# Two linear-attention and SwiGLU layers: gate and up of four column groups by two nested levels of seven block products instead of one

## The chip, the core and the metric

The kernel runs on one core of one Trainium2 chip, in one launch. The metric is the device time of a run in microseconds (us), as the median of several runs. Engine names are those of the profile: PE (TensorE matmuls), PEld (its weight loads), DVE (VectorE), ACT (ScalarE), POOL (GpSimd), SP (SyncE, which issues every DMA of this kernel). L947 is line 947 of the kernel's file.

## What is computed

Two equal layers are applied to x of 1 x 2048 x 512, one after the other; the weights are shared by the layers.

```python
x = x + A(layernorm(x), wqkv, wo)      # linear attention, 32 heads
x = x + B(layernorm(x), w1, w3, w2)    # SwiGLU MLP, F = 1792
x = x + A(layernorm(x), wqkv, wo)
x = x + B(layernorm(x), w1, w3, w2)

def B(x, w1, w3, w2):                  # x: 2048 x 512
    gate, up = x @ w1, x @ w3          # 512 x 1792 each
    return (silu(gate) * up) @ w2      # 1792 x 512
```

The change is in B of the second layer, "layer 1".

## The kernel before

**Numbers.** Every operand of a large matmul is held as two fp16 parts, a high part (the value rounded to fp16) and a low part (what is left). A product takes three matmul passes (`PASSES`: high x high, low x high, high x low), written by `mm` (L942, matmul at L947). So whoever makes an operand pays a rounding (ACT copy to fp16) and a subtraction (DVE or POOL, "low part").

**The MLP by seven products.** A product of two matrices, each cut into 2 x 2 blocks, can be made from seven block products instead of eight, if sums and differences of blocks stand ready on both sides (Winograd's form). P1 to P7 in the code name, for each of the seven products, which of the seven weight blocks or sums and which of the seven row blocks or sums it multiplies. Gate and up are made in this way: D = 512 is cut in two, the F columns in two, the tokens of a chunk in two. F is cut into seven **groups** (128 columns from each half of F, for w1 and for w3), the 2048 tokens into four **chunks** of 512 (as two halves of 256). The sums of weights and of rows are prepared ahead, in fp16 parts: the weights in layer 0 by `background`, a generator that is advanced a few steps after every group; the rows for each chunk by `mlp_rows` (L1963), which also writes them to DRAM (`xb_d`) for the later sets.

**A group** (`mlp_group`, L2029) is one group on one chunk: seven products x 2 weights x k = 2 x 3 passes = 84 matmuls of 128x256 into three PSUM banks, bb, ba and bc. The results are linear combinations of the products: ACT copies a bank to SBUF as it grows (L2052), DVE adds others to it (L2055, `a+`, `b+`, `c+`), so that the four quarters of gate and up arise. ACT makes the Silu (L2007) and DVE the gated product (L2008).

**The hidden values** (`hidden`, L2015) are cut for the down projection, which goes by seven products too: four sums of 128x256 (L2023 to L2026, on DVE or POOL, by a table), a high part on ACT (L2011) and a low part on DVE or POOL (L2013).

**Down** (`mlp_out`, L2087, matmul at L2097): for each group and each half of the chunk's rows, 42 matmuls of 128x256 that add up in four PSUM banks po0 to po3 over the groups of a set. At a set's end `mlp_add` (L2129) adds the banks to x: one ACT copy (L2148), five DVE operations that read po (L2146), and two adds in SBUF (L2154, L2155, on DVE or POOL by a table). The last group of all uses plain products (`mlp_out_plain`, L2106).

**Sets and slots.** `SETS` lists which groups run together; each set passes over the four chunks. Layer 0 has (0,1,2), (3,4), (5,6); layer 1 has (4,5,6), then (3,0,1,2). Prepared weights lie in SBUF slots of 14 KB (w1, w3) and 7 KB (w2) per partition; those that don't fit are written to DRAM (`store`) and fetched again (`fetch`).

**What sets the order.** In each engine the instructions run in the order of a written-out table `ORDER`, one list of numbers for each engine (PE, DVE, ACT, POOL, SP), which `arrange` (L679) imposes. So an instruction that waits holds up all that its list puts behind it. SP's list is the only DMA queue.

## Time and profile before

| | |
|---|---|
| median of 3 runs | 1136.95 us (1136.2 to 1137.05) |
| profiled execution: span | 1134.0 us |
| instructions | 22473 |
| PE busy | 1123.7 us, 9117 matmuls |
| DVE busy | 849.3 us |
| ACT busy | 663.2 us |
| POOL busy | 429.7 us |
| DMA | 162.94 MB, 144 GB/s in the mean |

The MLP of layer 0 runs from 186 to 561 us of the span, the attention of layer 1 to 753, the first set of layer 1's MLP to 904, its second set to 1109, and the last down projections to 1134. These borders are read from the adds from ba (L2055), of which there is one for each group and chunk. From 384.3 to 560.6 us are the last 13 of layer 0's 28 groups on chunks, from 752.9 to 903.7 the 12 of layer 1's first set, from 903.7 to 1108.9 the 16 of its second.

A row that groups instructions has line, engine, operation, names written and read, shapes and count, then busy us, the mean ns of one, and the engine's idle time just ahead of them with what ended it. A row of a single name or line has the shortest, median and longest duration in ns and the first and last start in us. A timeline row has start, duration (of the first start to the last end, where it stands for several), engine and operation, in brackets the idle time before it. In a table of stretches each engine's busy us stand with the number of instructions, then the granted TensorE clock, the busy share of the DMA engines and GB/s.

### The profile page before, as it was taken

How to read it: one execution, taken by the hardware profiler on the slowest of the kernel's cores; microseconds unless marked ns; L12 is line 12 of the kernel's file. 1: busy time of each engine (PE TensorE's matmuls, PEld its weight loads, DVE VectorE, ACT ScalarE, POOL GpSimd, SP SyncE). 2: the span in 40 equal slices, each digit the busy share in tenths (PEclk: the TensorE clock that was granted, in tenths of full speed). 3: DMA queues.
4: the chain of work that ended last, by engine and by line, in shares of the span. 5: the costliest groups of instructions: out<-in, count | busy, mean ns of one | idle time of the engine just before them, and what ended most of it. 6: DMA issues, size and time to landing. Idle time of an engine off the chain costs nothing.

```text
span 1134.0 us, 22473 instructions
## 1 busy us (share of the span) xinstructions
PE 1123.7 (99%) x9117; PEld 888.3 (78%) x9117; DVE 849.3 (75%) x1468; ACT 663.2 (58%) x1104; POOL 429.7 (38%) x477
## 2 busy tenths in 40 slices
PE   8999999999999999999999999999999999999998
PEld 3445446888888888888886676578888888888887
DVE  7789878896978887889896488847855666465556
ACT  7668878775544445455578666686544434343442
POOL 6731796502001222335678416862152110302113
PEclk9999999999999999999999999999999999999999
DMA  8995665389673332331267946643482440220001
GB/s 258 304 292 181 174 136 121 75 220 272 204 279 122 117 149 103 112 155 66 48 179 177 276 165 153 114 89 105 120 240 102 177 178 1 85 84 29 11 20 57
DMA packets 171768, 162.94 MB, mean 144 GB/s; under 512 B 139536, under 2 KB 147984, under 8 KB 167056
## 3 DMA queue, kind: packets, MB, share of 16 engines
q1 hardware_dynamic: 171664, 161.51, 48.7%
q8 instruction: 71, 1.16, 0.4%
q14 instruction: 33, 0.27, 0.1%
HBM read 80.08 MB, written 47.32 MB: 112 GB/s over the span
## 4 chain that ended last, share of the span: by engine, by line
PE 91%; DVE 2%; POOL 2%; DMA 2%; issue 1%; ACT 1%; SPq 0%; DVEq 0%; POOLq 0%; ACTq 0%
PE bb L947 26%; PE po L2097 20%; PE bc L947 13%; PE ba L947 6%; PE gt L947 6%; PE po L947 5%; PE pq L947 4%; PE pk L947 3%; PE po L2117 3%; DMA arena<-arena 2%; PE kb L947 1%; PE qb L947 1%; PE kc L947 1%; PE kv L947 0%; PE qc L947 0%
## 5 line engine op out<-in xcount | busy, mean ns | idle before, releaser
L947 PEld LDWEIGHTS <-arena 128*128 128x128 f16 x6648 | 646.1, 98 | 204.5 <-DMA arena<-arena 4.4
L947 PE MATMUL bb<-arena 128*128 128x256 f16 x2688 | 349.2, 273 | 0.0
L2097 PE MATMUL po<-arena 128*128 128x256 f16 x2058 | 288.5, 273 | 0.0
L2052 ACT ACTIVATE arena<-bb 128x512 f32<-128x512 f32 x196 | 115.3, 594 | 195.5 <-PE bb L947 166.7
L2097 PEld LDWEIGHTS <-arena 128*128 128x128 f16 x2058 | 201.3, 98 | 23.4
L947 PE MATMUL bc<-arena 128*128 128x256 f16 x1344 | 179.6, 273 | 0.0
L2055 DVE TENSOR_TENSOR arena<-arena,bc 128x512 f32<-128x512 f32 x112 | 76.7, 685 | 87.5 <-PE bc L947 54.1
L2007 ACT ACTIVATE arena<-arena,scalars 128x512 f32<-128x512 f32 x112 | 74.6, 666 | 90.2 <-DVE arena L2055 70.2
L2146 DVE SCALAR_TENSOR_TENSOR arena<-po,scalars,arena 128x256 f32<-128x256 f32 (+1 forms) x180 | 101.5, 585 | 31.7 <-PE po L2097 21.7
L2013 DVE TENSOR_TENSOR arena<-arena 128x1280 f16<-128x1280 f32 (+1 forms) x90 | 105.4, 1174 | 21.2 <-ACT arena L2011 20.8
L2011 ACT ACTIVATE arena<-arena 128x512 f16<-128x512 f32 (+1 forms) x112 | 101.0, 904 | 32.2 <-DVE arena L2026 13.7
L2008 DVE SCALAR_TENSOR_TENSOR arena<-arena,scalars 128x512 f32<-128x512 f32 x112 | 78.6, 705 | 34.5 <-ACT arena L2007 34.4
L947 PE MATMUL ba<-arena 128*128 128x256 f16 x672 | 91.8, 273 | 0.0
L947 PE MATMUL gt<-arena 128*128 128x512 f16 x384 | 89.6, 379 | 0.0
L947 PE MATMUL po<-arena 128*128 128x512 f16 x384 | 86.8, 379 | 0.5 <-DMA arena<-arena 0.5
L2013 POOL TENSOR_TENSOR arena<-arena 128x512 f16<-128x512 f32 x22 | 27.0, 1228 | 115.0 <-ACT arena L2011 108.2
L2155 POOL TENSOR_TENSOR arena<-arena 128x512 f32<-128x512 f32 x27 | 38.0, 1406 | 81.7 <-DVE arena L2146 81.7
L2154 POOL TENSOR_TENSOR arena<-arena 128x512 f32<-128x512 f32 x27 | 37.1, 1375 | 71.4 <-DVE arena L2146 69.3
L871 DVE SCALAR_TENSOR_TENSOR arena<-arena,scalars 128x512 f16<-128x512 f32 (+2 forms) x74 | 59.1, 814 | 2.3 <-ACT arena L869 2.2
L924 ACT ACTIVATE arena<-arena,nb_all,rs_all 128x512 f32<-128x512 f32 x64 | 50.8, 806 | 13.2 <-POOL nb_all L921 7.6
L2023 POOL TENSOR_TENSOR arena<-arena 128x256 f32<-128x256 f32 x10 | 7.9, 786 | 131.3 <-DVE arena L2008 131.3
L869 ACT ACTIVATE arena<-arena,scalars 128x512 f16<-128x512 f32 (+2 forms) x74 | 52.2, 718 | 5.2 <-DVE arena L1003 2.3
(234 smaller groups left out, 1449.4 us busy)
## 6 DMA issues: line engine op xcount, KB each, us to landing
arena<-xb_d SPq DMA_DIRECT2D x12, 1792.0 KB, 8.0
xb_d<-arena SPq DMA_DIRECT2D x8, 1792.0 KB, 7.7
w_d<-arena SPq DMA_DIRECT2D x5, 1792.0 KB, 7.6
arena<-w_d SPq DMA_DIRECT2D x5, 1792.0 KB, 8.0
arena<-in_B_w_dram SPq DMA_DIRECT2D x8, 896.0 KB, 7.0
arena<-in_B_w_dram SPq DMA_DIRECT2D x28, 256.0 KB, 3.0
xt_d<-arena SPq DMA_DIRECT2D x8, 896.0 KB, 5.1
arena<-xt_d SPq DMA_DIRECT2D x8, 896.0 KB, 6.7
```

Of the source, the lines that this page charges most:

```text
L869: nc.scalar.activation(hi, src, AF.Copy, scale=scale)
L871: lambda: nc.vector.scalar_tensor_tensor(lo, src, scale, hi, OP.mult, OP.subtract)
L924: nc.scalar.activation(dst, x_sb[:, t, :], AF.Identity, scale=rs_all[:, t : t + 1], bias=nb_all[:, t : t + 1],)
L947: nc.tensor.matmul(dst, lhs(a, k), rhs(b, k), start=first and k == 0 and i == 0, stop=last and k == n - 1 and i == len(PASSES) - 1, skip_g ...
L2007: nc.scalar.activation(t, gate, AF.Silu, scale=info["u1"])
L2008: nc.vector.scalar_tensor_tensor(t, up, info["hid"], t, OP.mult, OP.mult)
L2011: nc.scalar.activation(hs[:, 0, lo:hi], t[:, lo:hi], AF.Copy)
L2013: engine.tensor_tensor(hs[:, 1, lo:hi], t[:, lo:hi], hs[:, 0, lo:hi], OP.subtract)
L2052: nc.scalar.activation(dst, bank_, AF.Copy)
L2055: nc.vector.tensor_tensor(dst, dst, bank_, OP.add)
L2097: nc.tensor.matmul(po[:, i * HALF : (i + 1) * HALF], hs[:, a, qx, cs], w2[:, b, qw, :], start=g == ends[0] and i + a + b == 0, stop=g == e ...
L2146: nc.vector.scalar_tensor_tensor(dst, src, cb, to, OP.mult, OP.add)
```

## The change

Layer 1's MLP has one set of the old kind, the groups 0, 1 and 2. Groups 3 to 6 go as two **pairs**, (3,4) and (5,6), by a new function `unit49`: one unit is a pair on a chunk, and there are eight. The pair's 2 x 2 x 128 columns and the chunk's rows are cut twice, and the seven products are nested: an outer level of seven, and in each an inner seven, 49 products of 128 x 128 x 128 for each of w1 and w3. A unit's gate and up take 49 x 2 x 3 = 294 matmuls of 128x128 (before: 2 x 84 of 128x256). They run in four turns, each of two outer products (the last of one): in a turn the inner seven go through bb, ba and bc as before, with ACT copies and three DVE adds; then the outer combinations are made by seven DVE adds from bb in a unit and by seven `out_add`, each two POOL operations of 128x2x256 and 128x256 in SBUF. The gated products are four of 128x2x256 on DVE. Hidden values and the down projection stay as they are, on DVE throughout, and the down projection of a pair adds up over two groups, so that layer 1 has eight more calls of `mlp_add`.

The operands come from DRAM:
- `weights49` makes the sums of weights, as the last part of layer 0's background: 28 pieces, each with four sums of 128x128 in f32 and two low parts (128 and 256 wide) on POOL, three ACT copies, a low part of 128x512 on DVE and a write of 448 KB; besides 16 outer sums of 128x512 on POOL, 4 scalings on ACT and 16 loads of raw weights.
- `rows49` makes the sums of rows, in the hooks after the groups of layer 1's first set: for each chunk four scalings on ACT and four sums of 128x512 on POOL, and 28 pieces with four sums of 128x128 and a low part of 128x512 on DVE, two low parts (128 and 256 wide) on POOL, three ACT copies, a DMA transpose and a write of 448 KB.
- The units load 14 weight pieces of 896 KB and 56 row pieces of 448 KB, a unit ahead.

The weights of groups 0 to 2 (8 MB) are fetched again during layer 1's attention, where before two of them were fetched at the first set's end. `ORDER` is written anew.

By count of instructions: PE has 1344 fewer matmuls of 128x256 and 2352 more of 128x128. DVE has 112 more sums of 128x128, 56 more low parts of 128x512, 24 adds of 128x512 from ba in place of 16, 48 from bc in place of 32, 80 more adds of 128x256 from bb, ba and bc, 40 more steps of `mlp_add`, and 16 sums that POOL had. POOL has 168 more sums and low parts of 128x128, 56 low parts of 128x256, the 112 operations of `out_add`, 32 sums of 128x512 and 16 more of `mlp_add`.

The core of the diff:

```diff
-SETS = (((0, 1, 2), (3, 4), (5, 6)), ((4, 5, 6), (3, 0, 1, 2)))
+SETS = (((0, 1, 2), (3, 4), (5, 6)), ((0, 1, 2),))
+PAIRS = ((3, 4), (5, 6))
+TURNS = ((P1, P2), (P6, P7), (P5, P3), (P4,))
...
+    w49_d = dram.tile([P, 2, 7, 2, 14 * P], F16, name="w49_d")
+    x49_d = dram.tile([P, NC, 7, 14, P], F16, name="x49_d")
...
+        for pi in range(2):
+            yield from weights49(pi)
         while state["set"] < 2:
...
+    def fold(engine, at, sums):
+        b11, b21, b12, b22 = at
+        t1, t2, t3, t4 = sums
+        engine.tensor_tensor(t1, b12, b11, OP.subtract)
+        engine.tensor_tensor(t2, b22, t1, OP.subtract)
+        engine.tensor_tensor(t3, b22, b12, OP.subtract)
+        engine.tensor_tensor(t4, b21, t2, OP.subtract)
+
+    def weights49(pi):
...
+            def inner(o, src):
...
+                nc.gpsimd.tensor_tensor(s1, x21, x22, OP.add)
+                nc.gpsimd.tensor_tensor(s3, x11, x21, OP.subtract)
+                nc.gpsimd.tensor_tensor(s2, s1, x11, OP.subtract)
+                nc.gpsimd.tensor_tensor(s4, x12, s2, OP.subtract)
+                both = src[:, 1, :].rearrange("p (f n) -> p f n", f=2)
+                for lo, hi, part in ((0, 1, x11[:, None, :]), (1, 3, both), (3, 7, sums)):
+                    nc.scalar.activation(stage[:, 0, lo:hi, :], part, AF.Copy)
+                    (nc.vector if lo == 3 else nc.gpsimd).tensor_tensor(
+                        stage[:, 1, lo:hi, :], part, stage[:, 0, lo:hi, :], OP.subtract
+                    )
+                nc.sync.dma_start(w49_d[:, pi, o, w], stage.rearrange("p a i n -> p (a i n)"))
...
+    def rows49(c):
...
+        for pair_ in TURNS:
+            for _, qx in pair_:
...
+                fold(
+                    nc.vector, [src[:, i] for i in range(4)], [tau[:, i] for i in range(4)]
+                )
+                for lo, hi, part in ((0, 2, src[:, 0:2]), (2, 3, src[:, 3:4]), (3, 7, tau)):
+                    nc.scalar.activation(nat[:, 0, lo:hi, :], part, AF.Copy)
+                    (nc.vector if lo == 3 else nc.gpsimd).tensor_tensor(
+                        nat[:, 1, lo:hi, :], part, nat[:, 0, lo:hi, :], OP.subtract
+                    )
+                xt = turn49.next(F16, 14, P)
+                nc.sync.dma_start_transpose(xt, nat.rearrange("p a i n -> p (a i n)"))
+                nc.sync.dma_start(x49_d[:, c, qx], xt)
+                yield
...
+    def unit49(w49, x49, hs2, middle, plains):
...
+        def out_add(dst, a, b):
+            plus(nc.gpsimd, dst[:, 0:2], a[:, 0:2], b[:, 0:2])
+            plus(nc.gpsimd, dst[:, 3], a[:, 3], b[:, 3])
...
+        for at, os_ in enumerate(TURNS):
...
+            product(bb, os_, P1, True, False)
+            copy(one(0), src(bb))
+            product(bc, os_, P5, True, False)
+            product(bb, os_, P6, False, False)
+            copy(one(1), src(bb))
+            product(ba, os_, P2, True, True)
+            product(bb, os_, P7, False, False)
+            copy(one(3), src(bb))
+            plus(nc.vector, one(0), one(0), src(ba))
+            plus(nc.vector, one(3), one(3), src(bc))
+            product(bb, os_, P4, False, True)
+            product(bc, os_, P3, False, True)
+            middle(at)
+            plus(nc.vector, one(1), one(1), src(bc))
...
+        for i in range(2):
+            hidden(nc.vector, hs2[i], t49[:, i], None, plains[i])
```

Where the new order puts things shows best at three places. In the order's rows the lines of the changed kernel have other numbers: L2287 and L2288 are the two adds of `mlp_add` (before L2154 and L2155), L2146 the low part of the hidden values (L2013), L2188 the adds from ba and bc (L2055), L2141 the gated product (L2008), L2156 to L2159 the hidden sums (L2023 to L2026), L2279 the steps of `mlp_add` that read po (L2146).

First POOL's list in layer 0's last groups. Before (L1306 is an earlier part of the background):

```order
L1306 TENSOR_TENSOR arena<-arena 128x2x256 x4
L2155 TENSOR_TENSOR arena<-arena 128x512
L2013 TENSOR_TENSOR arena<-arena 128x512
L2154 TENSOR_TENSOR arena<-arena 128x512
L1306 TENSOR_TENSOR arena<-arena 128x2x256 x2
```

After; L1387 to L1390 are the inner sums of `weights49`, L1394 its low parts, L1408 its outer sums:

```order
L2146 TENSOR_TENSOR arena<-arena 128x512
L2287 TENSOR_TENSOR arena<-arena 128x512
L1390 TENSOR_TENSOR arena<-arena 128x128
L1388 TENSOR_TENSOR arena<-arena 128x128
L1394 TENSOR_TENSOR arena<-arena 128x256
L1394 TENSOR_TENSOR arena<-arena 128x128
L1408 TENSOR_TENSOR arena<-arena 128x512 x3
L1387 TENSOR_TENSOR arena<-arena 128x128
```

Between two operations that the groups need stand pieces of `weights49`.

Second DVE's list in layer 1's first set. Before:

```order
L2055 TENSOR_TENSOR arena<-arena,ba 128x512
L2013 TENSOR_TENSOR arena<-arena 128x512
L2025 TENSOR_TENSOR arena<-arena 128x256
L2024 TENSOR_TENSOR arena<-arena 128x256
L2026 TENSOR_TENSOR arena<-arena 128x256
L2055 TENSOR_TENSOR arena<-arena,bc 128x512
```

After; L1362 to L1365 are the sums of `fold`, L2115 to L2117 the sums of rows of the first set's next chunk:

```order
L2188 TENSOR_TENSOR arena<-arena,bc 128x512
L2115 TENSOR_TENSOR arena<-arena 128x256
L1362 TENSOR_TENSOR arena<-arena 128x128 x2
L2116 TENSOR_TENSOR arena<-arena 128x256
L2141 SCALAR_TENSOR_TENSOR arena<-arena,scalars 128x512
L1363 TENSOR_TENSOR arena<-arena 128x128
```

The small sums stand singly between the steps of the groups.

Third DVE's list in layer 1's last part. Before, in the second set:

```order
L2146 SCALAR_TENSOR_TENSOR arena<-po_11438,scalars,arena 128x512
L2023 TENSOR_TENSOR arena<-arena 128x256
L2024 TENSOR_TENSOR arena<-arena 128x256
L2025 TENSOR_TENSOR arena<-arena 128x256
L2146 SCALAR_TENSOR_TENSOR arena<-po_11436,scalars,arena 128x256 x2
```

After, in a unit; L2371 are the adds of the combinations, L2384 the gated product:

```order
L2279 SCALAR_TENSOR_TENSOR arena<-po_12048,scalars,arena 128x512
L2371 TENSOR_TENSOR arena<-arena,bc 128x512
L2384 SCALAR_TENSOR_TENSOR arena<-arena,pt_w_108 128x2x256
L2279 SCALAR_TENSOR_TENSOR arena<-po_12047,scalars,arena 128x256
L2371 TENSOR_TENSOR arena<-arena,bb 128x256
L2371 TENSOR_TENSOR arena<-arena,ba 128x512
```

Where hidden sums stood between the steps of `mlp_add`, there now stand adds from all three banks as well.

## The prediction

> **What bounds the kernel now.** First the profile's page: the busy shares and the slices.

> ```profile
> span 1134.0 us, 22473 instructions
> PE 1123.7 (99%) x9117; PEld 888.3 (78%) x9117; DVE 849.3 (75%) x1468; ACT 663.2 (58%) x1104; POOL 429.7 (38%) x477
> DVE  7789878896978887889896488847855666465556
> POOL 6731796502001222335678416862152110302113
> PEclk9999999999999999999999999999999999999999
> PE 91%; DVE 2%; POOL 2%; DMA 2%; issue 1%; ACT 1%; SPq 0%; DVEq 0%; POOLq 0%; ACTq 0%
> ```

> PE is busy for 99% of the span at full clock and holds 91% of the chain that ended last, so the kernel is bound by matmuls. The median of the runs, 1136.95 us, lies 2.95 us above this span. DVE and POOL have room on average, but not evenly. Next the table of stretches: layer 0's last groups, layer 1's first set, layer 1's second set.

> ```profile
> core 0: us, PE busy (x) PEld busy (x) DVE busy (x) ACT busy (x) POOL busy (x), PEclk, DMA share, GB/s
> 384.30:560.60 176.30, 176.30 (x1618) 158.01 (x1616) 152.30 (x260) 89.96 (x145) 70.87 (x63) 1.00 0.29 103
> 752.90:903.70 150.80, 150.80 (x1383) 135.09 (x1382) 102.02 (x164) 79.80 (x123) 46.10 (x42) 1.00 0.48 139
> 903.70:1108.90 205.20, 205.20 (x1882) 183.80 (x1881) 118.56 (x185) 85.28 (x128) 36.75 (x35) 1.00 0.17 64
> ```

> In all three PE never pauses. DVE is at 86%, 68% and 58%, POOL at 40%, 31% and 18%. The change takes work from PE in the third stretch and pays for it on DVE and POOL in all three, so the question is whether those two stay behind PE.

> **PE.** The list of PE waits has nothing from the MLP; its longest row comes from the end of the program:

> ```profile
> PE turn L2355 <- POOL arena L2361: 2.2, 1, 2.2
> 1117.85 6.93 PE L2097 MATMUL po<-arena 128*128 128x256 f16 x62
> 670.84 2.17 PE L947 MATMUL kv<-arena 128*128 128x128 f16 x36
> L947 PE MATMUL kv<-arena 128*128 128x128 f16 x96 | 6.0, 219 | 0.0
> L947 PE MATMUL bb<-arena 128*128 128x256 f16 x2688 | 349.2, 273 | 0.0
> L947 PEld LDWEIGHTS <-arena 128*128 128x128 f16 x6648 | 646.1, 98 | 204.5 <-DMA arena<-arena 4.4
> ```

> Sixty-two matmuls of 128x256 take 6.93 us in the timeline; less the 0.273 us of one, 109 ns from one to the next. Thirty-six of 128x128 take 2.17 us; less 0.219, 56 ns. A pair of groups on one chunk now costs 2 x (84 + 42) matmuls, 252 x 0.109 = 27.5 us. A unit of the change has 294 small ones and the same 84 down matmuls: 294 x 0.056 + 84 x 0.109 = 25.6 us. Eight units: 8 x (25.6 - 27.5), about **-16 us**. That is all that there is to gain.

> The 56 ns are open to one doubt: each of the kernel's 9117 matmuls has its own weight load, and one load lasts 98 ns. In the kv run they overlap. [...]

> **How DVE and POOL get in each other's way.** Shortest, median and longest duration of single operations, and one meeting in the timeline:

> ```profile
> L2023 DVE TENSOR_TENSOR arena<-arena x39: 411/424/1414, 284.7 to 1107.8; 128x256 f32<-128x256 f32 x39
> L2055 DVE TENSOR_TENSOR arena<-arena,bc x112: 673/687/689, 192.0 to 1118.2; 128x512 f32<-128x512 f32 x112
> L2023 POOL TENSOR_TENSOR arena<-arena x10: 723/730/1190, 348.1 to 1065.5; 128x256 f32<-128x256 f32 x10
> L2154 POOL TENSOR_TENSOR arena<-arena x27: 1267/1310/1713, 423.1 to 1127.5; 128x512 f32<-128x512 f32 x27
> L2013 DVE TENSOR_TENSOR arena<-arena x90: 677/1481/2376, 202.5 to 1123.4; 128x1280 f16<-128x1280 f32 x49, 128x512 f16<-128x512 f32 x41
> 1111.72 1.28 POOL L2155 TENSOR_TENSOR arena<-arena 128x512 f32<-128x512 f32 x1
> 1111.97 2.38 DVE L2013 TENSOR_TENSOR arena<-arena 128x1280 f16<-128x1280 f32 x1 [1.34 <-ACT arena L2011]
> ```

> A DVE operation with both inputs in SBUF is stretched up to threefold; one with an input in PSUM (bc) never is, in 112. In the timeline POOL's operation ends at 1113.00 and DVE's at 1114.35, 1.35 us later, though it needs 1.48 alone. So SBUF-to-SBUF operations of the two exclude each other, for all but some 0.14 us of each: I count "hold" as duration less 0.14. What has to fit into a stage is DVE's own load, and also the sum of both engines' holds.

> Prices, all from rows of single operations. DVE runs back to back about 0.08 us closer than its durations:

> ```profile
> 1101.10 0.69 DVE L2055 TENSOR_TENSOR arena<-arena,bc 128x512 f32<-128x512 f32 x1 [0.39 <-ACT arena L2052]
> 1101.71 0.68 DVE L2055 TENSOR_TENSOR arena<-arena,ba 128x512 f32<-128x512 f32 x1
> L1994 POOL TENSOR_TENSOR arena<-arena 128x256 f16<-128x256 f32 x9 | 6.0, 670 | 4.2 <-DMA arena<-arena 4.2
> ```

> So a 512-wide add costs DVE 0.60 (1101.10 to 1101.71), a 256-wide one 0.42 - 0.08 = 0.34. The 128-wide operations are not in the trace; carrying the line through 0.41 and 0.68 on gives DVE 0.28 (cost 0.20, hold 0.14), that through 0.72 and 1.27 gives POOL 0.46, and a 128-wide POOL low part is about 0.42 beside the 0.67 of a 256-wide. Their bounds are zero and the 256-wide rows.

> **Layer 0's last groups** (`weights49` as background). The DVE rows that read PSUM, by shape, from 384.3 to 560.6:

> ```profile
> L2146 DVE SCALAR_TENSOR_TENSOR arena<-po,scalars,arena 128x512 f32<-128x512 f32 x25 | 18.5, 746 | 5.9 <-PE po L2097 5.7
> L2055 DVE TENSOR_TENSOR arena<-arena,bc 128x512 f32<-128x512 f32 x27 | 18.5, 683 | 6.6 <-PE bc L947 4.4 <-ACT arena L2052 2.1
> L2146 DVE SCALAR_TENSOR_TENSOR arena<-po,scalars,arena 128x256 f32<-128x256 f32 x39 | 18.2, 477 | 1.6 <-POOL arena L2155 1.2
> L2055 DVE TENSOR_TENSOR arena<-arena,ba 128x512 f32<-128x512 f32 x13 | 8.8, 678 | 0.7 <-PE ba L947 0.7
> L2008 DVE SCALAR_TENSOR_TENSOR arena<-bb,scalars,arena 128x256 f32<-128x256 f32 x13 | 6.2, 478 | 1.7 <-ACT arena L2007 1.7
> ```

> They sum to 70.2, which leaves 82.1 us of SBUF work on DVE beside POOL's 70.9. Less 0.14 for each of 143 + 63 operations, the holds of today are 124 of 176.3 us. New on POOL are 28 pieces of 4 x 0.46 + 0.42 + 0.67 and 16 outer sums of 1.27: 102 us in 184 operations, 76 of hold; 20 of them stand before this stretch, so 68. New on DVE are 28 lows, 17 us of load (152.3 + 17 = 169, still below PE) and 28 x 0.55 = 15 of hold. Sum: 124 + 15 + 68 = 207 against 176, 31 over; some waiting is already in today's rows, twice, so I take **+26 us**, from +8 (DVE's small gaps absorb most) to +45. POOL and DVE work off lists in fixed order, in which the mlp_adds, hidden sums and lows that PE waits for stand between the pieces, so what is over lands on PE. The 84 ACT copies and the 28 writes of 448 KB have ACT at 51% and DMA at 29% for cover; without it a copy would cost its 0.3 to 0.6 us.

> **Layer 1's first set** (`rows49`), 752.9 to 903.7:

> ```profile
> L2055 DVE TENSOR_TENSOR arena<-arena,bc 128x512 f32<-128x512 f32 x23 | 15.8, 686 | 18.9 <-PE bc L947 13.6 <-ACT arena L2052 5.2
> L2146 DVE SCALAR_TENSOR_TENSOR arena<-po,scalars,arena 128x512 f32<-128x512 f32 x12 | 9.0, 748 | 3.5 <-PE po L2097 3.3
> L2146 DVE SCALAR_TENSOR_TENSOR arena<-po,scalars,arena 128x256 f32<-128x256 f32 x18 | 8.4, 479 | 4.5 <-PE po L2097 4.0 <-ACT arena L2148 0.5
> L2055 DVE TENSOR_TENSOR arena<-arena,ba 128x512 f32<-128x512 f32 x12 | 8.1, 679 | 7.4 <-PE ba L947 7.4
> ```

> PSUM rows 41.3, so SBUF work 60.7 in 99 operations, hold 47; POOL 46.1 in 42, hold 40. New: 112 folds x 0.14 + 28 x 0.55 = 31 on DVE; 28 x (0.42 + 0.67) + 16 x 1.27 = 50 on POOL, hold 40. Sum 158 against 150.8; DVE's load is 102 + 17 + 22 = 141. Slightly over, and packing two lists without gaps is not to be had: **+12**, from 0 to +25. The 28 transposes and 28 writes go through SP, the only issuing queue:

> ```profile
> L1989 SPq DMA_TRANSPOSE arena<-arena x16: 1295/1538/2506, 156.4 to 833.6; - x16
> w_d<-arena SPq DMA_DIRECT2D x5, 1792.0 KB, 7.6
> ```

> Between 1.3 and 2.5 us each, some 45 us of 151, with writes a quarter as large as the 7.6 us row: hidden. What SP carries late is the first unit's x49 loads, and the 8 MB that are now fetched inside the attention: 0 to +5 us, taken as 0.

> **The units.** By the new DVE list a unit has 9 adds of 512 from ba and bc, 3 of 256, 7 of 256 from bb, 4 gated products and 4.5 mlp_add steps of 512 (0.66), 6.8 of 256 (0.40), 8 sums (0.34), 2 lows of 1280 (1.40) and 1.5 of 512: about 23.5 us, below PE's 25.6. Holds on DVE: 8 x 0.28 + 2 x 1.34 + 1.5 x 0.54 + 4 x 0.61 = 8.2. On POOL 7 pairs of out_add (1.13 + 0.58) and 5.6 operations of 512 wide: 12.0 + 6.4 = 18.4. Together 26.6, over PE's 25.6, and DVE has only 2.1 us to wait in. I take 27.5 a unit, what it takes now: 8 x (27.5 - 25.6) = **+16**, which eats the gain. Bounds: 25.6 (0) and 30 (+35). ACT is busy for 85 of 205 us there now and DMA at 17%; the unit's copies and Silus, the 14 loads of 896 KB and the 56 of 448 KB fit beside PE, and cost nothing while a unit's x49 are fetched a unit ahead.

> The last unit's tail stays as it is: 0.

> **Sum.** 1134 - 16 + 26 + 12 + 16 = 1172 span; plus 2.95, **1175 us**.

> **Rivals.**
> - *Faster.* The background waits for DVE instead of DVE for it, and the holds interleave. Then PE stays the bound: 1134 - 16 + 3 = 1121, with small losses up to 1134. For it: no PE wait in the MLP today, 24 us of DVE gaps in layer 0's last groups. Against it: three sums over their limits. It decides at a hold demand of 176 us there and 25.6 in a unit. 0.22.
> - *Convoys, slower still.* Each new POOL operation costs the DVE operation behind it its whole hold. DVE would have 169 + 68 in layer 0, 141 + 40 in the first set, 23.5 + 12 in a unit: +61, +30 and, against 27.5 now, +64 over eight. Half of the 155 gives 1134 + 78 + 3 = 1215; 1205 to 1245. For it: 0.42 us operations stretched to 1.41. 0.13.
> - *Mostly hidden.* Only the lower bounds of layer 0 and half of the units' loss: -16 + 8 + 0 + 8 = 0, that is 1137, up to 1150: 0.04 for no change and 0.08 for a small loss.
> - *Weight loads not hidden.* At 98 ns a unit is 294 x 0.098 + 9.2 = 38 us, +84 over the eight, with the other stages' 38 about 1259. Against it the kv row; 0.03. [...]

> **Numbers.** The forecast, 1150 to 1205, has 0.50. Faster 0.22, same 0.04 (0.2% is about what a measurement of this kernel can tell from no change), slower 0.74. The range 1123 to 1222 leaves out some of the fastest case's end and the upper convoys.

> **What would show it.** In the new profile: PE busy per unit near 25.6 us in content, 56 ns from one 128-wide matmul to the next; layer 0's last groups longer than 176 us with PE idle behind DVE or POOL; SBUF rows on DVE (the sums, the lows) stretched well beyond 0.42 and 1.48, bc and ba rows unchanged at 0.68; a unit at 27 to 28 us. Wrong if PE stays at 99% throughout, or if PE waits mostly for DMA or SP.

## The result, and the profile after

The changed kernel takes 1286.4 us in the median (1284.1 to 1288.0), the kernel before 1137.0: a ratio of 1.1315, 95% interval 1.1299 to 1.1331. The forecast was 1175 with a range up to 1222. The direction holds; the loss is four times as large as forecast.

The page of the changed kernel:

```profile
span 1285.4 us, 25905 instructions
PE 1154.0 (90%) x10125; PEld 901.1 (70%) x10125; DVE 1104.0 (86%) x1801; ACT 758.1 (59%) x1341; POOL 782.4 (61%) x853
...
DVE  7799788977889879998975688799999788989988
POOL 6613985021046897988687038943774366767787
PEclk9999999999999989999999999999999999999998
PE 37%; DVE 31%; POOL 17%; issue 6%; ACT 5%; DMA 4%; SPq 0%; POOLq 0%; DVEq 0%; ACTq 0%
```

PE's share of the chain that ended last fell from 91% to 37%; DVE and POOL together now hold 48%. In POOL's slices the empty middle has filled. The table of stretches, for layer 0's last groups, layer 1's first set, the units, and the end:

```profile
core 0: us, PE busy (x) PEld busy (x) DVE busy (x) ACT busy (x) POOL busy (x), PEclk, DMA share, GB/s
390.90:622.80 231.90, 193.12 (x1613) 161.02 (x1611) 211.06 (x286) 123.47 (x226) 194.23 (x227) 0.96 0.46 165
815.80:1018.90 203.10, 168.39 (x1460) 142.77 (x1459) 187.08 (x305) 124.00 (x233) 114.32 (x123) 0.97 0.87 225
1018.90:1255.60 236.70, 209.31 (x2931) 195.78 (x2929) 212.19 (x334) 103.22 (x175) 170.78 (x141) 0.98 0.44 158
1255.60:1285.40 29.80, 17.54 (x138) 13.87 (x135) 24.84 (x36) 6.76 (x11) 20.90 (x15) 0.89 0.26 97
```

In the first three, DVE is now the busiest engine (91%, 92%, 90%), where PE was. The last groups of layer 0 went from 176 to 232 us, the first set from 151 to 203, and from the first unit to the end it takes 267 us where the second set and the end took 231. What PE waits for, by the list of waits:

```profile
PE bb L1021 <- ACT arena L2185: 34.4, 25, 3.5
PE po L2230 <- DVE arena L2279: 19.6, 22, 2.6
PE bc L1021 <- DVE arena L2371: 13.7, 14, 3.3
PE bc L1021 <- DVE arena L2188: 13.1, 10, 3.7
```

PE waits for banks that nobody has emptied in time: ACT's copy of bb waits for the SBUF place that DVE has not read yet (31 us of ACT's waits, L2185 on L2141), and mlp_add and the adds are DVE's own. DVE's rows by shape, layer 0's last groups:

```profile
L1394 DVE TENSOR_TENSOR arena<-arena 128x512 f16<-128x512 f32 x27 | 29.9, 1109 | 5.5 <-ACT arena L1393 5.4
L2146 DVE TENSOR_TENSOR arena<-arena 128x1280 f16<-128x1280 f32 x13 | 23.4, 1799 | 0.6 <-ACT arena L2144 0.4
L2279 DVE SCALAR_TENSOR_TENSOR arena<-po,scalars,arena 128x512 f32<-128x512 f32 x25 | 18.3, 739 | 1.1 <-PE po L2230 1.1
...
L2188 DVE TENSOR_TENSOR arena<-arena,bc 128x512 f32<-128x512 f32 x26 | 17.6, 675 | 0.5 <-PE bc L1021 0.4
...
L2158 DVE TENSOR_TENSOR arena<-arena 128x256 f32<-128x256 f32 x12 | 9.5, 791 | 0.1
```

The two rows that read PSUM (po, bc) are as before, 0.74 and 0.68. The three with both inputs in SBUF are stretched: 1.48 became 1.80, the sum of L2158 went from a mean of 0.46 (L2025 before) to 0.79, and a new low part, 0.68 where it meets nobody, takes 1.11. DVE's idle time in this stage hardly changed: 231.9 - 211.1 = 21 us, where it was 176.3 - 152.3 = 24. So the 59 us by which DVE's busy time grew did not go into its gaps; the stage became 56 us longer.

PE's own pace came as worked out. From the timeline of a unit:

```profile
1049.76 1.50 PE L1021 MATMUL bb<-arena 128*128 128x128 f16 x24 [0.73 <-ACT arena L2368]
```

(1.50 - 0.22) / 23 = 56 ns for each, with a new weight load each time (2929 loads beside the units' 2931 matmuls).

### The profile page after: what moved, and what is told of

Read it like the earlier page. It is cut to its first block, busy times and chain, and to the rows that moved or that the text cites. A ratio compares the mean times of both kernels' runs of the same rounds, so it can differ in the third digit from the quotient of the medians.

```text
span 1285.4 us, 25905 instructions
## 1 busy us (share of the span) xinstructions
PE 1154.0 (90%) x10125; PEld 901.1 (70%) x10125; DVE 1104.0 (86%) x1801; ACT 758.1 (59%) x1341; POOL 782.4 (61%) x853
## 4 chain that ended last, share of the span: by engine, by line
PE 37%; DVE 31%; POOL 17%; issue 6%; ACT 5%; DMA 4%; SPq 0%; POOLq 0%; DVEq 0%; ACTq 0%
PE bb L1021 7%; PE po L1021 5%; DVE arena L2146 5%; PE gt L1021 4%; POOL arena L2371 4%; DVE arena L2279 4%; PE bc L1021 3%; PE pq L1021 3%; PE pk L1021 3%; PE po L2230 3%; DMA arena<-arena 3%; PE po L2250 2%; DVE arena L2188 2%; DVE arena L2371 2%; DVE arena L2141 2%
## 5 line engine op out<-in xcount | busy, mean ns | idle before, releaser
L1021 PEld LDWEIGHTS <-arena 128*128 128x128 f16 x7656 | 673.9, 99 | 302.3 <-issue 99.6
L1021 PE MATMUL bb<-arena 128*128 128x256 f16 (+1 forms) x3264 | 366.0, 256 | 47.5 <-ACT arena L2185 34.4
L2230 PE MATMUL po<-arena 128*128 128x256 f16 x2058 | 309.8, 278 | 31.2 <-DVE arena L2279 19.6
L2230 PEld LDWEIGHTS <-arena 128*128 128x128 f16 x2058 | 198.4, 100 | 64.1 <-issue 26.8
L1021 PE MATMUL bc<-arena 128*128 128x256 f16 (+1 forms) x1632 | 188.2, 253 | 27.0 <-DVE arena L2371 13.7
L2371 POOL TENSOR_TENSOR arena<-arena 128x256 f32<-128x256 f32 (+1 forms) x112 | 127.6, 1159 | 62.5 <-DVE arena L2371 60.3
L2185 ACT ACTIVATE arena<-bb 128x512 f32<-128x512 f32 x132 | 77.7, 590 | 92.9 <-PE bb L1021 57.6
L2279 DVE SCALAR_TENSOR_TENSOR arena<-po,scalars,arena 128x256 f32<-128x256 f32 (+1 forms) x220 | 121.3, 580 | 9.3 <-ACT arena L2281 4.2
L2146 DVE TENSOR_TENSOR arena<-arena 128x1280 f16<-128x1280 f32 (+1 forms) x90 | 121.9, 1359 | 6.6 <-ACT arena L2144 6.3
L1021 PE MATMUL ba<-arena 128*128 128x256 f16 (+1 forms) x816 | 97.9, 253 | 9.2 <-DVE arena L2188 7.6
L2368 ACT ACTIVATE arena<-bb 128x512 f32<-128x512 f32 (+1 forms) x104 | 54.1, 529 | 84.4 <-PE bb L1021 70.5
L2140 ACT ACTIVATE arena<-arena,scalars 128x512 f32<-128x512 f32 x80 | 51.5, 643 | 66.3 <-DVE arena L2188 50.2
L2141 DVE SCALAR_TENSOR_TENSOR arena<-arena,scalars 128x512 f32<-128x512 f32 x80 | 61.3, 768 | 19.9 <-ACT arena L2140 19.8
L2334 POOL TENSOR_TENSOR arena<-arena 128x128 f16<-128x128 f32 (+1 forms) x56 | 40.1, 729 | 51.1 <-ACT arena L2333 47.9
L2188 DVE TENSOR_TENSOR arena<-arena,bc 128x512 f32<-128x512 f32 x80 | 54.3, 679 | 19.1 <-PE bc L1021 9.6
L2287 POOL TENSOR_TENSOR arena<-arena 128x512 f32<-128x512 f32 x35 | 55.0, 1571 | 20.5 <-DVE arena L2279 17.2
L2146 POOL TENSOR_TENSOR arena<-arena 128x512 f16<-128x512 f32 x22 | 28.7, 1308 | 56.2 <-ACT arena L2144 50.3
## 6 DMA issues: line engine op xcount, KB each, us to landing
xb_d<-arena SPq DMA_DIRECT2D x8, 1792.0 KB, 7.0
arena<-xb_d SPq DMA_DIRECT2D x8, 1792.0 KB, 8.3
```

What stands on the lines that cost most here:

```text
L1021: nc.tensor.matmul(dst, lhs(a, k), rhs(b, k), start=first and k == 0 and i == 0, stop=last and k == n - 1 and i == len(PASSES) - 1, skip_g ...
L2141: nc.vector.scalar_tensor_tensor(t, up, info["hid"], t, OP.mult, OP.mult)
L2146: engine.tensor_tensor(hs[:, 1, lo:hi], t[:, lo:hi], hs[:, 0, lo:hi], OP.subtract)
L2185: nc.scalar.activation(dst, bank_, AF.Copy)
L2188: nc.vector.tensor_tensor(dst, dst, bank_, OP.add)
L2230: nc.tensor.matmul(po[:, i * HALF : (i + 1) * HALF], hs[:, a, qx, cs], w2[:, b, qw, :], start=g == ends[0] and i + a + b == 0, stop=g == e ...
```

## The experiments

Each kernel below ran once, with a profile. Parts that a kernel does not touch came out within 3.5 us of the changed kernel's, so smaller differences cannot be told apart. In the diffs, `leave_out(engine)` drops an instruction and `add_after(engine, ...)` puts one into another engine's list; the order of all others stays. The theories: **exclusion** (what the prediction rests on), **load** (DVE's longer list is what costs, POOL is a bystander) and **lateness** (POOL's results come late to those who wait for them).

The stages in us, between the same adds from ba, and the time of the whole:

| kernel | whole | layer 0, first groups | layer 0, last groups | attention | first set | first unit to end |
|---|---|---|---|---|---|---|
| before | 1137.0 | 198.1 | 176.3 | 192.3 | 150.9 | 230.9 (second set) |
| changed | 1286.4 | 204.9 | 231.9 | 193.1 | 203.1 | 266.8 |
| w49_no_pool | 1254.3 | 203.7 | 197.8 | 192.1 | 204.1 | 268.8 |
| w49_no_dve | 1273.7 | 203.9 | 218.5 | 193.6 | 202.6 | 267.8 |
| w49_neither | 1242.8 | 202.8 | 189.3 | 192.3 | 203.3 | 267.2 |
| r49_no_pool | 1278.7 | 204.0 | 230.7 | 192.5 | 193.8 | 268.2 |
| r49_no_dve | 1264.7 | 202.8 | 231.7 | 192.4 | 182.0 | 268.1 |
| r49_copy | 1285.0 | 204.8 | 230.8 | 193.0 | 203.4 | 266.1 |
| r49_copy_no_dve | 1252.8 | 202.8 | 230.5 | 192.5 | 174.3 | 263.4 |
| unit_memset | 1258.6 | 204.1 | 230.7 | 192.3 | 202.7 | 241.2 |
| unit_no_outadd | 1257.3 | 203.0 | 232.0 | 192.8 | 203.2 | 238.6 |
| unit_outadd_dve | 1310.4 | 204.7 | 230.5 | 192.7 | 202.9 | 292.0 |
| unit_adds_out | 1259.0 | 202.9 | 230.5 | 192.5 | 202.5 | 242.3 |
| pe_and_copies | 1173.9 | 203.4 | 187.6 | 192.2 | 167.3 | 236.6 |
| no_copies | 1180.3 | 201.7 | 187.8 | 193.6 | 169.6 | 237.7 |
| few_dmas | 1177.5 | 203.5 | 186.1 | 194.0 | 169.5 | 236.3 |

### The two engines side by side: streams

Appended to the kernel before, behind its end:

```diff
+    def stretch(dve, pool):
+        nc.vector.tensor_tensor(a, p1, b, OP.add)
+        nc.gpsimd.tensor_tensor(p0, a, b, OP.add)
+        for i in range(48):
+            if dve:
+                dve(d0 if i % 2 else d1)
+            if pool and i % 3 == 0:
+                pool(p0 if i % 2 else p1)
...
+    stretch(sbuf(nc.vector, 256), None)
+    stretch(sbuf(nc.vector, 256), sbuf(nc.gpsimd, 512))
+    stretch(psum, sbuf(nc.gpsimd, 512))
+    stretch(sbuf(nc.vector, 256), fill)
+    stretch(sbuf(nc.vector, 256), sbuf(nc.gpsimd, 128))
```

> The kernel before, unchanged, and behind its end five stretches of 48 DVE adds of 128x256 with 16 POOL operations beside them (its time is longer for that and says nothing). Exclusion theory (an SBUF-to-SBUF operation of DVE and one of POOL shut each other out): DVE alone about 16 us; DVE with 16 POOL adds of 128x512 about 32 us, the sum of both holds, with the stretched DVE operations at 1.4 to 1.7 us; DVE reading PSUM with the same POOL adds about 20 us, POOL's own 16 x 1.27, and no DVE operation above 0.45; DVE with POOL fills, which read nothing, about 16 to 20 us; DVE with POOL adds of 128x128 about 20 us. Load theory (the engines do not disturb each other, DVE's own longer list is what costs): 16 to 20 us in all five.

The timeline (start, duration of the whole row):

```profile
1136.48 17.25 DVE L2444 TENSOR_TENSOR arena<-arena 128x256 f32<-128x256 f32 x48
1156.63 34.30 DVE L2444 TENSOR_TENSOR arena<-arena 128x256 f32<-128x256 f32 x48
1158.14 22.45 POOL L2444 TENSOR_TENSOR arena<-arena 128x512 f32<-128x512 f32 x16
1193.82 15.99 DVE L2447 TENSOR_TENSOR arena<-arena,bb 128x256 f32<-128x256 f32 x48
1195.09 19.61 POOL L2444 TENSOR_TENSOR arena<-arena 128x512 f32<-128x512 f32 x16
1217.53 17.25 DVE L2444 TENSOR_TENSOR arena<-arena 128x256 f32<-128x256 f32 x48
1219.02 7.51 POOL L2450 MEMSET arena<- 128x512 f32 x16
1237.74 21.38 DVE L2444 TENSOR_TENSOR arena<-arena 128x256 f32<-128x256 f32 x48
1239.25 9.53 POOL L2444 TENSOR_TENSOR arena<-arena 128x128 f32<-128x128 f32 x16
```

Each stretch begins with one more POOL add, so the first holds one meeting as well. Sixteen POOL adds of 512 cost DVE 34.30 - 17.25 = 17.05 us, 1.07 each out of the 1.23 that one takes beside DVE's reads of PSUM (19.61 / 16); beside DVE's SBUF adds POOL itself takes 22.5. With one input in PSUM, DVE takes 15.99 us beside the same POOL adds, no more than the first stretch's 17.25 less one meeting. Fills cost DVE nothing (17.25 again); adds of 128, 0.26 each ((21.38 - 17.25) / 16). The exclusion theory holds with its prices.

### Layer 0's last groups: w49_no_pool, w49_no_dve, w49_neither

```diff
-                nc.gpsimd.tensor_tensor(s1, x21, x22, OP.add)
...
+                leave_out("Pool", 4)
+                sums = ones[:, None, :].to_broadcast([P, 4, P])
...
+                    if lo == 3:
+                        nc.vector.tensor_tensor(
+                            stage[:, 1, lo:hi, :], part, stage[:, 0, lo:hi, :], OP.subtract
+                        )
+                    else:
+                        leave_out("Pool")
...
-                nc.gpsimd.tensor_tensor(to, x, y, op)
+                leave_out("Pool")
```

> Leaves out weights49's 184 POOL operations, so that the weights of the pairs are not the right ones; DVE, ACT, DMA and the order of all that is left stay. Exclusion theory: layer 0's last groups go from 232 us back to about 180 to 188, DVE's sums there from 0.77 to about 0.43, the whole to about 1240. Load theory: DVE's list is as long as before, so the stretch stays above 220 and the whole above 1272. Lateness theory (PE waits because POOL's own results come late): also about 180 to 188.

The second keeps POOL's and has `leave_out("DVE")` for the 28 low parts of 512; the third has both.

> Leaves out weights49's 28 low parts of 128x512 on DVE, so that the pairs' weights lack a part; POOL's 184 operations stay. DVE loses 17 us of work and 13 us of waiting. Exclusion theory: the stretch goes from 232 to 200 to 215, since each POOL operation still stops a DVE operation; the whole about 1260. Load theory: back to about 180, the whole about 1235. Lateness theory: 220 to 232, the whole above 1275.

> Leaves out both of weights49's parts, the 184 operations of POOL and the 28 low parts of DVE, so that the pairs' weights are not the right ones; ACT's copies, the loads of raw weights and the 28 writes stay. Layer 0's last groups: POOL's part alone was worth 34 us, DVE's alone 13. If DVE's list and what stops it are all there is, the two add up or overlap a little: 232 goes to 177 to 186. If the copies, the DMAs or the new order cost by themselves, it stays above 190.

Measured: 197.8, 218.5 and 189.3 us from 231.9. POOL's operations are worth 34 us, DVE's lows 13, both 43; 13 stay. None lies where exclusion or load alone had put it (180 to 188 or above 220; 200 to 215 or about 180; 177 to 186), and 218.5 is nearest to the 220 of lateness. Without POOL's part, DVE is still the fullest engine; first the stretch in the table, then two rows of DVE by shape:

```profile
389.70:587.60 197.90, 182.41 (x1615) 158.71 (x1613) 187.95 (x287) 122.19 (x226) 71.76 (x59) 0.98 0.55 195
```

```profile
L1421 DVE TENSOR_TENSOR arena<-ones,arena 128x512 f16<-128x512 f32 x27 | 23.5, 875 | 1.0 <-ACT arena L1419 1.0
...
L2187 DVE TENSOR_TENSOR arena<-arena 128x256 f32<-128x256 f32 x12 | 8.8, 736 | 0.1
```

POOL is busy for 72 us, as before the change, and yet DVE's sum (L2187 here) takes 0.74 where it took 0.46. So DVE and POOL can meet more often with no more work on POOL. With both parts out, as in pe_and_copies below, this shows without any new work on either:

```profile
388.50:576.10 187.60, 178.26 (x1619) 157.69 (x1617) 168.94 (x260) 121.68 (x227) 70.05 (x59) 1.00 0.58 207
```

DVE takes 169 us for 260 operations, where before it took 152 for 260, beside the same 70 us of POOL. In the trace of before, 15 of its 143 operations without an input in PSUM last over 0.15 us longer than the shortest of their shape; here it is 32 of 142, and in the changed kernel 108 of 169. Each of them has a POOL operation running beside it. It stays at 31 of 142 without ACT's copies (no_copies) and with half of the writes left out (few_dmas). So in the new order the same work of the two engines meets twice as often.

What these runs do not part is exclusion and lateness, since leaving POOL's operations out ends both. In the changed kernel ACT's copies of the pieces (L1393) wait for POOL's sums, and what stands behind them in ACT's list, bb's copies among it, waits with them:

```profile
ACT arena L1393 <- POOL arena L1390: 13.8, 9, 3.3
```

### Layer 1's first set: r49_no_pool, r49_no_dve, r49_copy, r49_copy_no_dve

```diff
-                fold(
-                    nc.vector, [src[:, i] for i in range(4)], [tau[:, i] for i in range(4)]
-                )
+                leave_out("DVE", 4)
+                tau = src
...
-                nc.sync.dma_start_transpose(xt, nat.rearrange("p a i n -> p (a i n)"))
+                nc.sync.dma_start(xt, nat.rearrange("p a i n -> p (a i) n"))
```

The first edit, with `leave_out` for the lows on DVE, is r49_no_dve; the second is r49_copy; r49_no_pool leaves out POOL's lows instead.

> Leaves out 52 of the 56 low parts that rows49 has on POOL, so that the rows lack a part; the 16 outer sums and everything on DVE, ACT and DMA stay. By the streams run a POOL add of 512 cost DVE 1.06 us and one of 128 about 0.26; 26 x (0.26 + 0.5) is about 20. Exclusion theory: layer 1's first set goes from 203 to about 183, the whole to about 1266. Load theory: 198 to 203.

> Leaves out rows49's work on DVE, 112 sums of 128x128 and 26 of 28 low parts of 128x512, so that the rows are not the right ones; all of POOL, ACT and DMA stay. Load theory: the first set goes from 203 back to PE's 151 to 155, the whole to about 1236. Exclusion theory: POOL's 40 us of holds still stop DVE, 155 to 170, the whole 1240 to 1250.

Measured: 193.8 and 182.0 from 203.1. DVE's part is worth 21 us, POOL's lows 9. Both theories named other times (183 or 198 to 203; 155 to 170 or 151 to 155). POOL's 16 outer sums, of which the prediction had 16 x 1.27 = 20 us, stay in all of these kernels. With DVE's part out, another figure stands out, a DMA share of 0.98:

```profile
812.90:994.90 182.00, 163.14 (x1448) 140.31 (x1447) 124.18 (x173) 123.10 (x234) 112.51 (x123) 0.98 0.98 249
```

So the next two asked whether the transposing DMAs are the bound.

> The 28 transposing DMAs of rows49 become plain copies of the same size, so that the rows are not the right ones; all else stays. DMA theory (the transposes fill the DMA engines, ACT waits for a free buffer and PE for ACT): the DMA share of layer 1's first set falls from 0.87 to about 0.55; DVE with its 187 busy us stays, so the set goes from 203 to 188 to 196. If only DVE's list counts: 200 to 203.

> As the one before, and rows49's sums and low parts on DVE are left out as well. Without DVE's part but with the transposes the set took 182 us at a DMA share of 0.98. DMA theory: now 152 to 160, PE's own time. If the rest was POOL's doing: 175 to 182.

Measured: 203.4 with copies alone, though the DMA share fell from 0.87 to 0.68; and 174.3 with DVE's part out too. The DMA theory falls for the changed kernel: behind a full DVE the transposes cost nothing, and without it 8 us.

### The units: unit_memset, unit_no_outadd, unit_outadd_dve, unit_adds_out

```diff
 # unit_memset
-            plus(nc.gpsimd, dst[:, 0:2], a[:, 0:2], b[:, 0:2])
-            plus(nc.gpsimd, dst[:, 3], a[:, 3], b[:, 3])
+            nc.gpsimd.memset(dst[:, 0:2], 0.0)
+            nc.gpsimd.memset(dst[:, 3], 0.0)
 # unit_no_outadd
+            leave_out("Pool", 2)
 # unit_outadd_dve
+            leave_out("Pool", 2)
+            add_after("DVE", mine, lambda: plus(nc.vector, dst[:, 0:2], a[:, 0:2], b[:, 0:2]))
+            add_after("DVE", mine, lambda: plus(nc.vector, dst[:, 3], a[:, 3], b[:, 3]))
```

> In the units POOL fills the results of out_add with zeros in place of adding, so that the result is not the right one; the writes and what waits for them stay, the reads go, and a fill may be shorter than an add. Exclusion theory, if a fill does not shut DVE out: DVE's sums in the units go from 0.49 to 1.06 us down to 0.42 to 0.45, the units with the tail from 267 to about 230, the whole about 1250. If a fill does shut it out, the gain is only what the fill is shorter. Load theory: the same 267 as now, for DVE's list is as long. Lateness theory: between 240 and 267, by how much shorter a fill is.

> Leaves out the 112 out_adds on POOL, so that the result is not the right one; DVE, ACT, PE and DMA stay. With fills in their place the part from the first unit to the end took 241 us (267 in the changed kernel). Exclusion theory: about the same, 236 to 242, for the fills did not stop DVE. Lateness theory: clearly less than 236, since now nobody waits for POOL's results. Load theory: 267.

> The out_adds go from POOL to DVE, each right behind the adds that it needs; nothing is left out. A unit's DVE list grows by 7 x (0.60 + 0.34) = 6.6 us, from 23.5 to 30.1, and POOL's list loses 14 us. Load theory: DVE sets a unit's time, so eight units are some 50 us longer, the whole about 1335. Exclusion theory: on POOL the seven pairs cost DVE 7 x (1.06 + 0.5) = 10.9 us of waiting, so the part from the first unit on is 0 to 30 us shorter than 267, the whole 1256 to 1286.

Measured, from the first unit to the end: 241.2, 238.6 and 292.0, from 266.8. Fills, which still wait for DVE and are waited for, give back 26 of the 28 us that leaving the adds out gives. DVE's busy time from the first unit on falls with them from 237 us to 216, so most of that is exclusion. Lateness is not ruled out for the rest: a fill lasts 0.53 and 0.31 us, far less than an add, so POOL's results come earlier too. In the changed kernel ACT waits 28 us for the out_adds, with fills 2:

```profile
ACT arena L2383 <- POOL arena L2371: 14.9, 18, 2.1
ACT arena L2368 <- POOL arena L2371: 13.6, 6, 3.5
```

Two rows of DVE by shape, in the changed kernel's units (without the tail) and then with fills (with the tail):

```profile
L2384 DVE SCALAR_TENSOR_TENSOR arena<-arena,pt_w 128x512 f32<-128x512 f32 x29 | 30.0, 1034 | 4.8 <-ACT arena L2383 4.8
...
L2156 DVE TENSOR_TENSOR arena<-arena 128x256 f32<-128x256 f32 x14 | 14.7, 1061 | 0.0
```

```profile
L2384 DVE SCALAR_TENSOR_TENSOR arena<-arena,pt_w 128x512 f32<-128x512 f32 x32 | 28.6, 897 | 1.5 <-ACT arena L2383 1.4
...
L2156 DVE TENSOR_TENSOR arena<-arena 128x256 f32<-128x256 f32 x16 | 10.4, 661 | 0.1
```

The sums and gated products shorten, but the sums not to 0.42; mlp_add's two adds, which stay on POOL, are there to meet them. On DVE the out_adds cost 292.0 - 238.6 = 53 us, their own 8 x 6.6; on POOL only 28. My expectation for that kernel (1256 to 1286) failed: in the units DVE is so full that each us put on it is a us of time, and POOL is the cheaper place even with the exclusion. It had charged POOL's adds their full 10.9 us a unit; the trace gives 28 / 8 = 3.5.

With the out_adds gone the units still take 8 us more than the second set before, with less work for PE. The last unit kernel took the adds from bb off DVE as well (`moved` puts an ACT copy in their place):

```diff
+        def moved(dst, a, b):
+            leave_out("DVE")
+            add_after("Activation", mine, lambda: copy(dst, b))
...
-                plus(nc.vector, each[0][:, 2], keep["o1"][:, 2], last_(bb, 0))
+                moved(each[0][:, 2], keep["o1"][:, 2], last_(bb, 0))
```

> As unit_no_outadd (out_adds left out), and the 56 adds of 128x256 from bb go off DVE: ACT copies in their place, the sums are left out. DVE loses 56 x 0.34 = 19 us, ACT gets 56 x 0.47 = 26. If DVE's list still sets the units' time: from the first unit to the end 239 goes to 220 to 230, the whole about 1242. If PE or the end of the program sets it: 235 to 239.

It took 242.3, more than either theory had named: DVE's list no longer sets the time there. What does is open; ACT has some 26 us more to do in this kernel.

### What stays: pe_and_copies, no_copies, few_dmas

The first joins the edits shown above: POOL's and DVE's part of both preparations and the out_adds left out, copies for transposes. The second leaves out ACT's copies of the pieces too (`leave_out("Activation")`), the third most of their DMAs:

```diff
+                if c == 0:
+                    nc.sync.dma_start(xt, nat.rearrange("p a i n -> p (a i) n"))
+                    nc.sync.dma_start(x49_d[:, c, qx], xt)
+                else:
+                    leave_out("SP", 2)
```

> Leaves out everything that the preparation of weights and rows puts on DVE and POOL (but for the scalings, the rows' 16 outer sums and the first two pieces) and the out_adds, with plain copies for the transposes; what is left of the change is PE's smaller work, ACT's copies, the units' adds on DVE and the DMAs. From the runs so far: 203 early or less, 177 to 186, 193, 152 to 160, and 239 from the first unit on, behind a start of 186: 1145 to 1167. If PE's 16 us come through in full once nothing stops DVE, the last part is 231 or less and the whole 1125 to 1140.

> As pe_and_copies, and ACT's copies of the pieces are left out too (but for the first two of the rows), so that of weights49 and rows49 only scalings, outer sums of the rows, DMAs and the order of the rest are left. If ACT's copies hold PE up: layer 0's last groups 188 to 177-180, the first set 167 to 157-160, the whole about 1153. If it is the order or the DMAs: 186 to 188, 165 to 167, the whole about 1170.

> As no_copies, and the copies and writes of the rows' pieces are left out for three of the four chunks, the writes of the weights' pieces for the second pair (the units load what is there). If the DMAs hold what is left of the loss: the first set 170 to 156-160, layer 0's last groups 188 to about 182. If it is the order of the lists: 167 to 170 and 186 to 188.

Measured: 1173.9, 1180.3 and 1177.5. The first two lie above every time named for the whole; by its stages the third fits the order of the lists (167 to 170 and 186 to 188). So 106 to 113 of the changed kernel's 149 us go with DVE's and POOL's new operations and what follows from them. At least 37 us stay, and since PE has 15 us less to do, some 52 are lost elsewhere. In pe_and_copies these are 5 in layer 0's first groups, 11 in its last groups, 16 in the first set (of which some 5 are PE's own: 1449 matmuls between the same adds in place of 1383, 59 of them small), and in the units 6 besides their saving.

- First groups: 3.5 us are a single wait, found in every kernel with the new order (2.1 to 3.6 us). In the changed kernel a scaling of raw weights (L1378) has ACT wait 3.60 us for a DMA from 303.9 us on, and bb's copy, for which PE waits 3.43 us, stands behind it. The granted clock then is 0.50 for 3.4 us.
- Last groups: it is neither ACT's copies (187.6 and 187.8) nor the writes that few_dmas leaves out (186.1). DVE needs 17 us more for the same work, as shown above, so the new order acts at least in part through the same exclusion.
- First set: neither ACT's copies (167.3 and 169.6) nor three quarters of the rows' DMAs (169.5) make it up. But POOL is still busy for 80 us there, 46 before, the 16 outer sums among it. These were not taken out.
- Units: DVE keeps the new adds from the banks. Taking those from bb off as well gained nothing (unit_adds_out).

That the rest is the order of the lists is argued, not shown, since the old order cannot be kept with the new instructions.

## Why the prediction was wrong, step by step

**PE: right.** The pace is 56 ns, the loads of 98 ns in the trace of before hidden; 2352 x 0.056 - 1344 x 0.109 = -15 us of matmul time did come (the prediction's -16 is rounded too far). The rival with exposed weight loads, at 98 ns a matmul, is not seen.

**The exclusion: right, and priced right for one meeting.** 1.07 us of DVE for a POOL add of 512 against a hold of 1.13; 0.26 for one of 128 against 0.32. PSUM reads go free, as read from the 112 rows (673 to 689 ns); in streams 48 DVE adds of 128x256 that read PSUM took 15.99 us beside POOL's adds.

**"DVE's load 169, still below PE": the step that failed.** I set DVE's load and the sum of holds beside the length of a stage, each for itself, and took only what was over: 26, 12 and 16 us. That supposes that everything below the limit fits into gaps. But DVE works off one list. Its time in a stage is its load plus every wait, and waits came about where it reached an SBUF operation while POOL had one running (108 of 169 operations in the last groups, as shown above), however far the sums were from the limit. In the last groups DVE's busy time grew by 59 us, of which 17 are the new lows, and the stage by 56; of DVE's 24 us of gaps, 21 are still gaps. I had put DVE's own additions at nothing, in the last groups and in the first set both; w49_no_dve and r49_no_dve give 13 and 21 us for them, out of loads of 17 and 38 (112 x 0.20 + 26 x 0.60). In the units the out_adds on DVE cost 53 for 53. POOL's cost comes on top: 34, 9 and 28.

**A full DVE is not needed for it.** In w49_no_dve DVE is busy for 182 of 218 us, 83% and less than the 86% of before, and the stage is still 42 us longer than before. That a load stays below the length of the stage says nothing of what POOL costs.

**POOL's share.** Of 68 us of new holds in layer 0's last groups, 34 ended on PE; of about 20 for the lows of the first set, 9; of 8 x 12 in the units, 28. So a POOL operation cost from 0.3 to half of its hold, with what its lateness costs in it. The rival "convoys" charged all of it, +155, and halved that; a half rate is about right for POOL in the first two. That its full +155 lies near the measured +151 is chance: it had nothing for DVE's additions, the clock and the order.

**Transposes "hidden": right only behind DVE.** I priced them by the 1.3 to 2.5 us of their issue; the DMA engines' share rose to 0.87. It would have been the next bound, at 8 us (182.0 against 174.3 with DVE's part out).

**Not foreseen: the clock, up to 26 us**, told below, which goes with PE's pauses; and the some 52 us that stay when most of DVE's and POOL's new work is gone. The prediction put layer 0's first groups at nothing; they became 7 us longer, and 5 of these are the wait for a DMA with the slow clock behind it, where DMA and ACT had been taken as covered.

**The units.** Forecast +16 over PE's own time, measured about +50: from the first unit on PE has 2283 matmuls of 56 ns and 783 of 109, 213 us, against 2080 of 109 before, 227; that is 14 less, and the time is 36 more. The out_adds account for 28. For the rest the PE waits speak for the shorter products: "PE bc <- DVE" and "PE bb <- ACT" with 14 and 9 waits in the units, where before there were none. A product of twelve matmuls, which gives ACT the time for its 0.59 us copy, now lasts 0.67 us in place of 1.31. This was not tried.

## What to carry to other kernels

Before moving work to a helper engine, add up the load of the engine that shares data with it, with its waits, over the stage in which it runs: a load below the length of the stage does not mean that there is room. Here DVE in fixed order, busy for 68% and 83% of a stage without its new work (r49_no_dve, w49_no_dve), turned half and four fifths of that work into time, and at 89% (unit_no_outadd) all of it. A saving of 15 us on the busiest engine was not worth a preparation that puts 56 us on DVE and 153 on POOL, however idle they look on average. Where DVE and POOL exclude each other, let the one read PSUM, or let the other only write: in streams DVE's 48 adds took 34.30 us beside POOL's adds, 15.99 with an input in PSUM and 17.25 beside fills.

## What the runs showed of the hardware

**A pause of PE can cost twice.** The granted clock was 1.00 in all three stretches of the table of before and fell to 0.96 in layer 0's last groups. The timeline around one pause:

```profile
408.48 0.82 PE L1021 MATMUL ba<-arena 128*128 128x256 f16 x6
411.32 0.81 PE L1021 MATMUL bc<-arena 128*128 128x256 f16 x6 [2.02 <-DVE arena L2188]
411.98 1.32 PE L1021 MATMUL bb<-arena 128*128 128x256 f16 x6
413.09 2.13 PE L2230 MATMUL po<-arena 128*128 128x256 f16 x9
415.01 1.09 PE L1021 MATMUL bc<-arena 128*128 128x256 f16 x6
```

PE waits 2.02 us for DVE, runs six matmuls at full pace, and from about 412.2 to 415.4 it takes 213 ns for each in place of 109 (nine in 2.13 us). So the pause costs another 1.6 us. The trace has fifteen such phases before its end, one of them twice as long, each in or just behind a pause of 1.8 to 4.1 us. By the mean granted clock, 0.979 of 1285.4 us against 0.999 of 1134.0, they took up to 27 us of PE's time, where before it was 1.

```profile
408.72:412.13 3.41, 1.39 (x14) 1.09 (x12) 3.41 (x4) 0.76 (x2) 3.41 (x5) 1.00 0.18 20
412.14:415.55 3.41, 3.41 (x18) 2.43 (x17) 3.41 (x5) 3.41 (x8) 3.33 (x6) 0.50 0.71 269
951.44:954.86 3.42, 2.45 (x23) 2.04 (x21) 3.38 (x5) 2.58 (x6) 3.42 (x5) 1.00 0.89 205
954.86:958.27 3.41, 1.67 (x14) 1.35 (x14) 3.41 (x6) 0.00 (x0) 3.41 (x5) 1.00 0.49 199
```

In the first pair PE was idle for 2.02 us of one window, and the next ran at 0.50. In the second pair the pause lay across a border, 0.97 and 1.74 us, and no slow window followed. Of the windows at full clock in this trace, the fifteen that a slow one followed had at least 1.93 us of PE idle, all others at most 1.80; in the trace of before, the one had 2.06 and all others at most 1.58. So here a window that was idle for little more than half was enough.

**The exclusion slows both sides.** POOL's sixteen adds took 22.5 us beside DVE's stream and 19.6 beside DVE operations that read PSUM; DVE's stream took 34.3 us beside them and 17.25 in the first stretch, with one POOL add.
